# Turning filter rows with permutation matmuls instead of DRAM row moves, with later V loads and spread weight transposes

## Chip, cores, metric

The program runs on one core of one Trainium2 chip. The metric is the device time of one execution in microseconds (us). A ratio below is the mean time of one kernel's fast runs over that of the other's of the same rounds, so it is not quite the ratio of the medians quoted beside it.

## The reference, cut to what matters

```python
def _A_ref(x, w_r, w_i):                  # x: (1, 2048, 576)
    X = rfft2(x.astype(float32))          # (2048, 289) complex
    return irfft2(X * (w_r + 1j * w_i))   # filter: 2048 x 289

def _B_ref(x, w_gate, w_up, w_down):      # 576 -> 4608 -> 576
    return (gelu(x @ w_gate) * (x @ w_up)) @ w_down

g = sigmoid((x * gate_w).sum(-1))
out = g * _A_ref(x) + (1 - g) * _B_ref(x)
# wanted: out, and the gradients of x, w_r, w_i, w_gate, w_up, w_down, gate_w
```

The kernel does the Fourier transforms as matmuls. They are cut into small "units" and laid between the matmuls of the wide layer, so that TensorE (PE) always has work. The other engines are VectorE (DVE), ScalarE (ACT), GpSimd (POOL) and SyncE (SP), which issues the DMAs here.

## The kernel before

The wide layer has 18 groups of 256 hidden columns. Each group has four quarters (m = 0 to 3, 512 rows each), so there are 72 quarters; I count them from 0. A quarter begins with the matmuls `z` that read the transposed down-weights `wdT`.

By symmetry of the transform the kernel works on columns 0 to 144 of a row and meets columns 145 to 288 of the mirrored row there (row S - s for row s). So the right half of the filter has to be there in mirrored row order, and the right half of its gradient has to be put back. The kernel before does both through DRAM, on SP's queue:

```python
def reversed_rows(src, dst, tiles):
    s_, d_ = (a.rearrange("(m i) (h l) -> h i m l", i=T, h=2) for a in (src, dst))
    ...
    out.append(lambda i=i: LD.dma_start(d_[:, i], s_[:, T - i, ::-1]))   # LD = nc.sync
# main loop, end of a quarter
if m < 3 and g + 1 < NG:
    load_w(g + 1, m)            # part m of the next group's weights, also on SP
...
for _ in range(5 if pr < 8 else 2):
    if moves:
        moves.pop(0)()          # row moves, on SP
```

The middle of the transform, per pair of rows p, and the pool of "unit" buffers that it lives from (19 buffers, shared by everything named here):

```python
def prefetch(p):                # V tiles (vx, vg) and the filter tile W
    st[p, "vx"] = load_V(scr_x, i0); st[p, "vg"] = load_V(scr_g, i0)
    w = unit([2, 2, DF], name="Wt") ...
def s2(p, which, ii):           # last forward step: PE, then ACT, DVE
    ...
    if which == "g" and ii == 1:
        side.extend(products(p))        # 12 DVE items: m1 m2 qm n1 n2 qn o1 o2
        if p + 1 < T // 2: prefetch(p + 1)
def s1(p, key, ii, dst):        # first inverse step
    ...                                 # four matmuls into vps
    Vt = unit([2, 2, HF], name="Vt")    # a unit buffer
    nc.scalar.copy(Vt..., vps...)       # ACT drains PSUM
    LD.dma_start(dst..., Vt...)         # store
```

From group 1 on, `z` and all transform units share one PSUM buffer (pool `pz`, one buffer), which ACT drains; `da` is the tile that ACT writes when it drains `z`. Pairs of rows are worked on one after another: one turn of the middle takes the last forward steps of pair p and the first inverse steps of pair p - 1.

Of the kernel before, what the change touches and what calls it, by code (L numbers as in the profile page):

```python
# [9 lines left out]
ACT = mybir.ActivationFunctionType  # L10
# [53 lines left out]
def iotas(nc, res, unit):  # L64
    tb = Tables()
    G = nc.gpsimd
    kw = dict(allow_small_or_imprecise_dtypes=True)
    tb.lrow = unit([HF], F32, name="lrow")
    G.iota(tb.lrow[:], pattern=[[1, HF]], base=0, channel_multiplier=0, **kw)
    tb.dcol = res.tile([P, 5], F32, name="dcol")  # L70
    for par in range(2):
        G.iota(tb.dcol[:, 2 * par:2 * par + 2], pattern=[[256, 2]], base=par, channel_multiplier=2, **kw)
    G.iota(tb.dcol[:, 4:5], pattern=[[0, 1]], base=512, channel_multiplier=1, **kw)
    tb.dn = res.tile([P, 5], F32, name="dn")
    nc.vector.tensor_scalar(tb.dn[:], tb.dcol[:], 1.0 / D, None, op0=ALU.mult)
    tb.krow = res.tile([P, P], F32, name="krow")
    G.iota(tb.krow[:], pattern=[[1, P]], base=0, channel_multiplier=0, **kw)
    tb.scol = res.tile([P, T], F32, name="scol")
    G.iota(tb.scol[:], pattern=[[1, T]], base=0, channel_multiplier=16, **kw)
    tb.mrow_i = res.tile([P, P], I32, name="mrow_i")  # L80
    G.iota(tb.mrow_i[:], pattern=[[1, P]], base=0, channel_multiplier=0)
    tb.qcol_i = res.tile([P, 1], I32, name="qcol_i")
    G.iota(tb.qcol_i[:], pattern=[[0, 1]], base=0, channel_multiplier=1)
    par_i = res.tile([P, 1], I32, name="par_i")
    nc.vector.tensor_single_scalar(par_i[:], tb.qcol_i[:], 1, op=ALU.bitwise_and)
    tb.par = res.tile([P, 2], F32, name="par_f")
    nc.vector.tensor_copy(tb.par[:, 1:2], par_i[:])
    nc.vector.tensor_scalar(tb.par[:, 0:1], tb.par[:, 1:2], -1.0, 1.0, op0=ALU.mult, op1=ALU.add)
    tb.halfpi = res.tile([P, 1], F32, name="halfpi")
    nc.vector.memset(tb.halfpi[:], math.pi / 2)  # L90
    tb.pi = res.tile([P, 1], F32, name="pi")
    nc.vector.memset(tb.pi[:], math.pi * EPS_SCALE)
    tb.npi = res.tile([P, 1], F32, name="npi")
    nc.vector.memset(tb.npi[:], -math.pi * EPS_SCALE)
    tb.warm = res.tile([P, 1], F32, name="warm")
    nc.scalar.activation(tb.warm[:], tb.halfpi[:], ACT.Sin)
    tb.late = []
    tb.Dt = []
    return tb
# [86 lines left out]
def kernel(  # L186
# [22 lines left out]
    scr = [[dram.tile([TPB, P, FF], BF16, name=f"scr{k}_{tp}") for tp in range(NT)] for k in range(3)]  # L209
    a_scr = dram.tile([S, D], BF16, name="a_scr")  # L210
    dxa_scr = dram.tile([S, D], BF16, name="dxa_scr")
    wrev, orev = ([dram.tile([S, DF - HF], BF16, name=f"{n}{k}") for k in range(2)] for n in ("wrev", "orev"))
    scr_x = dram.tile([T, P, 2, 2 * HF], BF16, name="scr_x")
    scr_g = dram.tile([T, P, 2, 2 * HF], BF16, name="scr_g")
    scr_p1 = (dram.tile([T, P, 2, 256], BF16, name="scr_p1"), dram.tile([2, T, P, 2, NL // 2], BF16, name="scr_q1"))
# [45 lines left out]
        load_x(4 * k)  # L261
    for k in range(4):
        load_do(4 * k)
    for part in range(3):
        load_w(0, part)
    gwb = res.tile([P, D], BF16, name="gwb")

    ew = wstack.enter_context(tc.tile_pool(name="ew", bufs=2))
# [15 lines left out]
    omg32 = res.tile([P, T], F32, name="omg32")  # L284
    tb.Rt = []
    tb.At2 = hres.tile([P, 2, 2, 2 * HF], BF16, name="At2")
    tb.Oi = hres.tile([P, 2, HF], BF16, name="Oi")

    hctr = [0]
# [92 lines left out]
        V.tensor_tensor(q[:], xb[:], q[:], op=ALU.mult)  # L382
        return xb, q, s, hu

    stores, moves = [], []

    def flush(n=9):

# [156 lines left out]
    def tail_table():  # L545

        n = HF - P
        nc.gpsimd.memset(tb.At2[:], 0.0)
        tp_ = pz.tile([P, 2, 1024], BF16, tag="z", name="tp")
        for c in range(2):  # L550
            nc.tensor.transpose(tp_[:, c, 0:P], tb.Dt[2][:, c, 0:P], ident[:])
            nc.tensor.transpose(tp_[0:n, c, 256:256 + P], tb.Dt[2][:, c, P:HF], ident[:])
            nc.tensor.transpose(tp_[:, c, 512:512 + 32], tb.Dt[3][0:32, c, 0:P], ident[0:32, 0:32])
            nc.tensor.transpose(tp_[0:n, c, 768:768 + 32], tb.Dt[3][0:32, c, P:HF], ident[0:32, 0:32])
        V.tensor_copy(tb.Oi[:, :, 0:P], tp_[:, :, 0:P])
        V.tensor_copy(tb.Oi[:, :, P:HF], tp_[:, :, 512:512 + n])
        ot = unit([2, HF], name="ot")
        V.tensor_copy(ot[0:n, :, 0:P], tp_[0:n, :, 256:256 + P])
        V.tensor_copy(ot[0:n, :, P:HF], tp_[0:n, :, 768:768 + n])
        for i in range(2):  # L560
            LD.dma_start(tb.At2[i * NL:i * NL + n, i, :, 0:HF], tb.Dt[1][0:n])
            LD.dma_start(tb.At2[i * NL + n:(i + 1) * NL, i, :, HF:2 * HF], ot[0:n])
# [14 lines left out]
    wi_v = A_w_i.rearrange("(m i) l -> m i l", i=T)  # L577
    o2v = out_2.rearrange("(m i) l -> m i l", i=T)
    o3v = out_3.rearrange("(m i) l -> m i l", i=T)
    def tiles_of(t):  # L580
        return t[:].rearrange("(m i) l -> m i l", i=T)

    def reversed_rows(src, dst, tiles):

        s_, d_ = (a.rearrange("(m i) (h l) -> h i m l", i=T, h=2) for a in (src, dst))
        out = []
        for i in tiles:
            if i:
                out.append(lambda i=i: LD.dma_start(d_[:, i], s_[:, T - i, ::-1]))
            else:  # L590
                out.append(lambda: LD.dma_start(d_[:, 0, 1:P], s_[:, 0, P - 1:0:-1]))
                out.append(lambda: LD.dma_start(dst[0:1], src[0:1]))
        return out

    a_dv = a_scr[:].rearrange("(m i) d -> m i d", i=T)
    dxa_dv = dxa_scr[:].rearrange("(m i) d -> m i d", i=T)

    def mid_units():
        st = {}

        def prefetch(p):
            i0 = 2 * p
            st[p, "vx"] = load_V(scr_x, i0)
            st[p, "vg"] = load_V(scr_g, i0)
            w = unit([2, 2, DF], name="Wt")
            for k, v in enumerate((wr_v, wi_v)):
                LD.dma_start(w[:, k, :, 0:HF], v[:, i0:i0 + 2, 0:HF])
                LD.dma_start(w[:, k, :, HF:DF], tiles_of(wrev[k])[:, i0:i0 + 2, :])
            nc.gpsimd.tensor_scalar(w[:, 1, :, HF:DF], w[:, 1, :, HF:DF], -1.0, None, op0=ALU.mult)
            st[p, "w"] = w  # L610

        def s2(p, which, ii):
            def f():
# [14 lines left out]
                V.tensor_tensor(o[:, ii, :, DF - 1:HF - 1:-1], xe[:, :, 0:HF - 1], xe[:, :, HF:w - 1], op=ALU.subtract)  # L628
                if which == "g" and ii == 1:
                    side.extend(products(p))  # L630
                    if p + 1 < T // 2:
                        prefetch(p + 1)
            return f

        def products(p):
# [32 lines left out]
                return f  # L668

            def out_dw():  # L670
                o = st[p, "o1"]
                nc.gpsimd.tensor_scalar(o[:, :, 1, HF:DF], o[:, :, 1, HF:DF], -1.0, None, op0=ALU.mult)

                def store():
                    for k, v in enumerate((o2v, o3v)):
                        LD.dma_start(v[:, i0:i0 + 2, 0:HF], o[:, :, k, 0:HF])
                        LD.dma_start(tiles_of(orev[k])[:, i0:i0 + 2, :], o[:, :, k, HF:DF])
                        moves.extend(reversed_rows(orev[k][:], (out_2, out_3)[k][:, HF:DF], [(T - i) % T for i in (i0, i0 + 1)]))
                stores.append(store)
            return [  # L680
                lambda: halve(G),
                mul("m1", X, W[:, 0]), mul("m2", X, W[:, 1]), comb("m1", "m2", False),
# [6 lines left out]
        def s1(p, key, ii, dst):  # L689
            def f():  # L690
                i = 2 * p + ii
                while (p, key + "_q") not in st:
                    side.pop(0)()
                Pt = st[p, key + "_q"][:].rearrange("p i c e l -> p i c (e l)")
# [18 lines left out]
        NPAIR = T // 2  # L713
        for p in range(NPAIR + 1):
            if p < NPAIR:
                out += [s2(p, "x", 0), s2(p, "x", 1), s2(p, "g", 0), s2(p, "g", 1)]
            else:
                out += [gap] * 3
            if p > 0:
                out += [s1(p - 1, "m1", 0, scr_p1), s1(p - 1, "m1", 1, scr_p1)]  # L720
                out += [s1(p - 1, "n1", 0, scr_p2), s1(p - 1, "n1", 1, scr_p2)]
        return out

    def inv_units(s, dv, scale):
# [82 lines left out]
    run_late(tb)  # L807
    for t in range(T):
        x1[t]()
        if t % 4 == 2 and t < 14:  # L810
            tchunk(xn, xT, t + 2)
        if t >= 9 and t % 2 == 1:
            tchunk(dB, dOT, 2 * (t - 9))
        if t % 3 == 1 and t + 2 < T:
            build_R(nc, tb, unit, t + 2)
        if tb.late:
            tb.late.pop(0)()
        if t > 1:
            x2[t - 2]()
    x2[T - 2]()  # L820
    build_B(nc, tb, unit, res)
    run_late(tb)
    for i in range(T):
        for k, v in enumerate((A_w_r, A_w_i)):
            moves.extend(reversed_rows(v[:, HF:DF], wrev[k][:], [i]))
    x2[T - 1]()
    gate()

# [57 lines left out]
    for g in range(NG):  # L886
# [3 lines left out]
        for m in range(NPR):  # L890
# [4 lines left out]
            hs = [h for u in pend[m] for h in u] if pend else []  # L895

            def side_work():
                for _ in range(4):
                    if side:
                        side.pop(0)()  # L900
            if g == 0 and m > 0:
# [55 lines left out]
                LD.dma_start(gwb[:], gate_w.partition_broadcast(P))  # L957
            if (g, m) in ((0, 3), (1, 0)):
                scale_dB(T // 2)
            for _ in range(5 if pr < 8 else 2):  # L960
                if moves:
                    moves.pop(0)()
            assert pr != 8 or not moves
            if done[0] == n_slots or (pr >= wgT_from and pr % 2 == 0 and len(wgT_all) < 20):
                load_wgT()
                if done[0] == n_slots:
# [1 line left out]
        carry = pend[4] if pend else []  # L968
        pend = W_units(g)
    flush()  # L970
    assert fft_pos[0] == len(fft) and not side and not moves
    hstack.close()


# [225 lines left out]
```

## Time and profile before

| | before |
|---|---|
| time | 1493.15 us (1492.37 to 1493.29, 3 runs) |
| PE busy | 1413.8 us of 1492.2 |
| PE waits for `wdT` | 31.3 us, four times, at quarters 4 and 8 |
| PE waits behind ACT in the middle | 7.1 us for `da`, 5.7 us for `Vt` |

How to read it: what can be won is PE's idle time, and besides it the time that PE loses in matmuls at a low granted clock after a long wait ("slow clock" below), which the page counts as busy. The head is the time before quarter 0, the end stage that after the last quarter. A PE wait is listed with the engine, the tile and the line that ended it. "ACT Vt" means that PE waited for ACT to drain the transform's result and free the PSUM buffer. The lines are in the prediction.

### The profile page before, as it was taken

The numbers are of one execution on the slowest core, as the hardware profiler recorded it, in microseconds if no ns is written. First come the engines' busy times: TensorE is split into PE (matmuls) and PEld (weight loads), VectorE is DVE, ScalarE is ACT, GpSimd is POOL, SyncE is SP. The second block draws the span as 40 slices with busy tenths as digits, with TensorE's granted clock in tenths as the row PEclk, the third lists the DMA queues.
The fourth block names the chain that finished last, engine by engine and source line by source line (L and its number), as shares of the span: only waits on it lengthen the run. The fifth ranks groups of instructions, "written<-read, shape, count | busy, mean of one in ns | idle before, by whom it ended". The sixth has DMA issues, their size and how long they took to land.

```text
span 1492.2 us, 30025 instructions
## 1 busy us (share of the span) xinstructions
PE 1413.8 (95%) x11500; PEld 1050.0 (70%) x11586; DVE 886.3 (59%) x2356; ACT 695.5 (47%) x1380; POOL 136.1 (9%) x224
## 2 busy tenths in 40 slices
PE   7959599899999999999999999999999999999997
PEld 5637367666766676677777777777877777777776
DVE  6767277988888888876777777776000561212110
ACT  5846366576677666767677667664000000000000
POOL 1000011111111111010010010011000110000000
PEclk9979799999999999999999999999999999999999
DMA  5234364355555564456445546565999997877773
GB/s 194 67 85 104 92 183 135 105 122 144 137 135 135 137 158 110 116 135 152 122 124 141 151 125 163 142 155 138 268 208 200 209 211 159 167 161 163 156 153 73
DMA packets 555891, 217.63 MB, mean 146 GB/s; under 512 B 380868, under 2 KB 545860, under 8 KB 555748
## 3 DMA queue, kind: packets, MB, share of 16 engines
q1 hardware_dynamic: 546116, 195.21, 57.4%
q0 software_dynamic: 7824, 19.49, 4.5%
q8 instruction: 90, 1.47, 0.4%
q10 hardware_dynamic: 1808, 1.02, 0.3%
q14 instruction: 53, 0.43, 0.1%
HBM read 43.28 MB, written 96.22 MB: 93 GB/s over the span
## 4 chain that ended last, share of the span: by engine, by line
PE 57%; issue 0%; DVE 0%; ACT 0%; DVEq 0%
PE acc L1047 28%; PE wps L464 8%; PE xy L353 7%; PE wps L447 5%; PE z L341 4%; PE wps L477 1%; PE pf L748 1%; PE xy L348 1%; PE z L344 1%; PE pf L775 1%; PE pf L777 1%; PE pf L761 0%; ACT da L366 0%; DVE n L649 0%; PE pf L698 0%
## 5 line engine op out<-in xcount | busy, mean ns | idle before, releaser
L1047 PEld LDWEIGHTS <-pin 128*128 128x128 bf16 x3456 | 338.1, 98 | 85.1
L353 PE MATMUL xy<-wgu,xT 128*128 128x512 bf16 x1066 | 256.3, 379 | 10.6 <-issue 9.1
L464 PEld LDWEIGHTS <-xn 128*128 128x128 bf16 x2304 | 225.2, 98 | 31.2 <-issue 0.2
L353 PEld LDWEIGHTS <-xT 128*128 128x128 bf16 x1152 | 106.6, 98 | 138.8 <-issue 31.5
L366 ACT ACTIVATE da<-z,omg 128x256 bf16<-128x256 f32 x288 | 113.0, 474 | 150.0 <-PE z L344 147.1
L341 PE MATMUL z<-wdT,dOT 128*128 128x256 bf16 x1152 | 142.5, 278 | 37.6 <-DMA wdT<-wtmp 31.3
L1064 ACT COPY bo<-acc 128x288 f32<-128x288 f32 x32 | 12.7, 398 | 308.1 <-PE acc L1047 250.0
L341 PEld LDWEIGHTS <-dOT 128*128 128x128 bf16 x1152 | 112.8, 99 | 58.0 <-DMA wdT<-wtmp 32.1
L447 PE MATMUL wps<-dB,A 128*128 128x288 bf16 x1152 | 152.7, 286 | 0.0
L1047 PE MATMUL acc<-wgT,pin 128*128 128x288 bf16 x1152 | 143.6, 286 | 0.0
L1047 PE MATMUL acc<-wuT,pin 128*128 128x288 bf16 x1152 | 143.6, 286 | 0.0
L1047 PE MATMUL acc<-wd_all,pin 128*128 128x288 bf16 x1152 | 142.6, 286 | 0.0
L447 PEld LDWEIGHTS <-A 128*128 128x128 bf16 x1152 | 112.6, 98 | 34.9
L464 PE MATMUL wps<-dHg,xn 128*128 128x256 bf16 x1152 | 133.1, 273 | 0.0
L464 PE MATMUL wps<-dHu,xn 128*128 128x256 bf16 x1152 | 132.0, 273 | 0.0
L1124 DVE SCALAR_TENSOR_TENSOR f32t<-gwf,dlog,b16t 128x576 f32<-128x576 f32 x16 | 13.1, 818 | 176.7 <-DMA b16t<-dxa_scr 176.7
L372 ACT ACTIVATE q<-xy 128x512 bf16<-128x512 f32 x144 | 86.2, 598 | 65.8 <-PE xy L353 62.0
L396 ACT ACTIVATE om<-s 128x512 bf16<-128x512 bf16 x144 | 92.1, 640 | 22.6 <-DVE s L380 22.3
L397 ACT ACTIVATE s<-s 128x512 bf16<-128x512 bf16 x144 | 90.7, 630 | 4.6
L470 POOL DMA_DIRECT2D out_dram<-dw x67 | 48.9, 730 | 458.5 <-ACT dw L425 336.9
L379 DVE TENSOR_SCALAR s<-q 128x512 bf16<-128x512 bf16 x144 | 42.5, 295 | 80.8 <-ACT q L372 80.1
L378 ACT CAST hu<-xy 128x512 bf16<-128x512 f32 x144 | 87.2, 606 | 0.0
(209 smaller groups left out, 1803.9 us busy)
## 6 DMA issues: line engine op xcount, KB each, us to landing
scr<-A SPq DMA_DIRECT2D x144, 128.0 KB
scr<-dHg SPq DMA_DIRECT2D x144, 128.0 KB
scr<-dHu SPq DMA_DIRECT2D x144, 128.0 KB
out_dram<-dw POOLq DMA_DIRECT2D x67, 128.0 KB, 2.8
wd_all<-in_B_w_down_dram SPq DMA_DIRECT2D x3, 1728.0 KB
out_dram<-dwd POOLq DMA_DIRECT2D x34, 144.0 KB, 3.1
wgu<-in_B_w_gate_dram SPq DMA_DIRECT2D x18, 256.0 KB
wgu<-in_B_w_up_dram SPq DMA_DIRECT2D x18, 256.0 KB
```

What stands on the lines that cost most here:

```text
L341: nc.tensor.matmul(zo(t), lhsT=dOT[:, ci, t, :], rhs=wdT[:, ci, :], start=(t % 4 < 2 and ci == 0), stop=False)
L353: nc.tensor.matmul(xy[k][:, t % 2, :], lhsT=xT[:, ci, t, :], rhs=wgu[:, ci, :], start=False, stop=(ci == 3))
L366: nc.scalar.activation(da[:, tt, :], z[:, tt, k, :], ACT.Copy, scale=omg32[:, t:t + 1])
L372: nc.scalar.activation(q[:], xy[:, :, 0:FG], ACT.Square)
L378: nc.scalar.copy(hu[:], xy[:, :, FG:2 * FG])
L379: V.tensor_scalar(s[:], q[:], A_GELU, 1.0, op0=ALU.mult, op1=ALU.add)
L396: nc.scalar.activation(om[:], s[:], ACT.Sigmoid, scale=-2.0 * C_GELU)
L397: nc.scalar.activation(s[:], s[:], ACT.Sigmoid, scale=2.0 * C_GELU)
L447: nc.tensor.matmul(wps[:, :288], lhsT=tl(0, t)[:, fch * P:(fch + 1) * P], rhs=dB[:, t, h * 288:(h + 1) * 288], start=(t == 0), stop=(t == ...
L464: nc.tensor.matmul(wps[:, cc, :], lhsT=xn[:, t, (c0 + cc) * P:(c0 + cc + 1) * P], rhs=tl(k, t), start=(t == 0), stop=(t == T - 1))
L470: wst[0].dma_start(ov[:, c0:c0 + TPB, fsl], dw[:])
L1047: nc.tensor.matmul(acc[:, :288], lhsT=src[:, r, :], rhs=w_of(r)[:, h * 288:(h + 1) * 288], start=(first and r == 0), stop=(last and r == F ...
```

## The change

The intent: take the row moves out of SP's queue. Loads and stores fetch and put the mirrored row inside each block of 16 rows directly. Only the order of the 128 partitions is left to be turned, and a matmul with a permutation matrix J does that, in place (a "flip"). Beside this: weight transposes are issued later in the head, V and filter loads later, and the DVE side work goes three items at a time.

```diff
-    for part in range(3):
-        load_w(0, part)
+    load_w(0, 0)
 ...
+        if t in (6, 11):                       # in the head's loop
+            load_w(0, 1 + t // 11)
 ...
+        def flip(p, of):
+            ps = pftile()
+            for k in range(2):
+                for ii in range(2):
+                    nc.tensor.matmul(ps[:, k, ii * (HF - 1):(ii + 1) * (HF - 1)], lhsT=tb.J[:, int(p == ii == 0), :],
+                                     rhs=of(k)[:, ii if p == 0 else 1 - ii, HF:DF], start=(ii == 0), stop=(ii == 1))
+            for k in range(2):
+                nc.scalar.activation(of(k)[:, :, HF:DF], ps[...], ACT.Copy, scale=(1.0, -1.0)[k])
 ...
-                LD.dma_start(w[:, k, :, HF:DF], tiles_of(wrev[k])[:, i0:i0 + 2, :])
-            nc.gpsimd.tensor_scalar(w[:, 1, :, HF:DF], w[:, 1, :, HF:DF], -1.0, None, op0=ALU.mult)
+                for sb, d in mirrored(w[:, k], v, p):
+                    LD.dma_start(sb, d)
 ...
-                    if p + 1 < T // 2:          # in s2
+                    if p == 0:
                         prefetch(p + 1)
+                if key == "m1" and ii == 1 and p + 2 < T // 2:   # in s1
+                    prefetch(p + 2)
 ...
-                out += [s2(p, "x", 0), s2(p, "x", 1), s2(p, "g", 0), s2(p, "g", 1)]
+                out += [flip_w(p), s2(p, "x", 0), s2(p, "x", 1), s2(p, "g", 0), s2(p, "g", 1)]
 ...                                             # and flip_o(p - 1) after the four s1
-                for _ in range(4):              # side_work
+                for _ in range(3):
 ...
-            for _ in range(5 if pr < 8 else 2):
-                if moves:
-                    moves.pop(0)()
```

More of the change, by code (lines that the diff above doesn't have):

```diff
@@ L88, in iotas @@
     nc.vector.tensor_scalar(tb.par[:, 0:1], tb.par[:, 1:2], -1.0, 1.0, op0=ALU.mult, op1=ALU.add)
+    tb.rcol = res.tile([P, 2], F32, name="rcol")
+    G.iota(tb.rcol[:], pattern=[[1, 2]], base=P - 1, channel_multiplier=-1, **kw)
     tb.halfpi = res.tile([P, 1], F32, name="halfpi")
@@ L211 @@
     dxa_scr = dram.tile([S, D], BF16, name="dxa_scr")
-    wrev, orev = ([dram.tile([S, DF - HF], BF16, name=f"{n}{k}") for k in range(2)] for n in ("wrev", "orev"))
     scr_x = dram.tile([T, P, 2, 2 * HF], BF16, name="scr_x")
@@ L286 @@
     tb.At2 = hres.tile([P, 2, 2, 2 * HF], BF16, name="At2")
+    tb.J = hres.tile([P, 2, P], BF16, name="J")
     tb.Oi = hres.tile([P, 2, HF], BF16, name="Oi")
@@ L383, in H_ew1 @@
         return xb, q, s, hu
-    stores, moves = [], []
+    stores = []
     def flush(n=9):
@@ L548, in tail_table @@
         nc.gpsimd.memset(tb.At2[:], 0.0)
+        for k in range(2):
+            V.tensor_scalar(tb.J[:, k, :], tb.krow[:], tb.rcol[:, k:k + 1], None, op0=ALU.is_equal)
+        nc.gpsimd.memset(tb.J[0:1, 1, 0:1], 1.0)
         tp_ = pz.tile([P, 2, 1024], BF16, tag="z", name="tp")
@@ L579 @@
     o3v = out_3.rearrange("(m i) l -> m i l", i=T)
-    def tiles_of(t):
-        return t[:].rearrange("(m i) l -> m i l", i=T)
-    def reversed_rows(src, dst, tiles):
-        s_, d_ = (a.rearrange("(m i) (h l) -> h i m l", i=T, h=2) for a in (src, dst))
-        out = []
-        for i in tiles:
-            if i:
-                out.append(lambda i=i: LD.dma_start(d_[:, i], s_[:, T - i, ::-1]))
-            else:
-                out.append(lambda: LD.dma_start(d_[:, 0, 1:P], s_[:, 0, P - 1:0:-1]))
-                out.append(lambda: LD.dma_start(dst[0:1], src[0:1]))
-        return out
     a_dv = a_scr[:].rearrange("(m i) d -> m i d", i=T)
@@ L599, in mid_units, with mirrored, flip_w, flip_o @@
         st = {}
+        def mirrored(sb, v, p):
+            hi = slice(HF, DF)
+            if p == 0:
+                return [(sb[:, 0, hi], v[:, 0, hi]), (sb[:, 1, hi], v[:, T - 1, hi])]
+            return [(sb[:, :, hi], v[:, T - 1 - 2 * p:T + 1 - 2 * p, hi])]
+        def flip(p, of):
[4 more added lines that the diff above has]
+                                     rhs=of(k)[:, ii if p == 0 else 1 - ii, HF:DF], start=(ii == 0), stop=(ii == 1))
+            for k in range(2):
+                nc.scalar.activation(of(k)[:, :, HF:DF], ps[:, k, :DF - 1].rearrange("p (i l) -> p i l", i=2), ACT.Copy,
+                                     scale=(1.0, -1.0)[k])
+        def flip_w(p):
+            return lambda: flip(p, lambda k: st[p, "w"][:, k])
+        def flip_o(p):
+            def f():
+                while (p, "o1_ready") not in st:
+                    side.pop(0)()
+                o = st[p, "o1"]
+                flip(p, lambda k: o[:, :, k, :])
+                def store():
+                    for k, v in enumerate((o2v, o3v)):
+                        LD.dma_start(v[:, 2 * p:2 * p + 2, 0:HF], o[:, :, k, 0:HF])
+                        for sb, d in mirrored(o[:, :, k, :], v, p):
+                            LD.dma_start(d, sb)
+                stores.append(store)
+            return f
         def prefetch(p):
@@ L630, in f @@
                     side.extend(products(p))
-                    if p + 1 < T // 2:
+                    if p == 0:
                         prefetch(p + 1)
@@ L670, in out_dw @@
             def out_dw():
-                o = st[p, "o1"]
-                nc.gpsimd.tensor_scalar(o[:, :, 1, HF:DF], o[:, :, 1, HF:DF], -1.0, None, op0=ALU.mult)
-                def store():
-                    for k, v in enumerate((o2v, o3v)):
-                        LD.dma_start(v[:, i0:i0 + 2, 0:HF], o[:, :, k, 0:HF])
-                        LD.dma_start(tiles_of(orev[k])[:, i0:i0 + 2, :], o[:, :, k, HF:DF])
-                        moves.extend(reversed_rows(orev[k][:], (out_2, out_3)[k][:, HF:DF], [(T - i) % T for i in (i0, i0 + 1)]))
-                stores.append(store)
+                st[p, "o1_ready"] = True
             return [
@@ L720, in mid_units @@
                 out += [s1(p - 1, "m1", 0, scr_p1), s1(p - 1, "m1", 1, scr_p1)]
-                out += [s1(p - 1, "n1", 0, scr_p2), s1(p - 1, "n1", 1, scr_p2)]
+                out += [s1(p - 1, "n1", 0, scr_p2), s1(p - 1, "n1", 1, scr_p2), flip_o(p - 1)]
         return out
@@ L822 @@
     run_late(tb)
-    for i in range(T):
-        for k, v in enumerate((A_w_r, A_w_i)):
-            moves.extend(reversed_rows(v[:, HF:DF], wrev[k][:], [i]))
     x2[T - 1]()
@@ L959 @@
                 scale_dB(T // 2)
-            for _ in range(5 if pr < 8 else 2):
-                if moves:
-                    moves.pop(0)()
-            assert pr != 8 or not moves
             if done[0] == n_slots or (pr >= wgT_from and pr % 2 == 0 and len(wgT_all) < 20):
@@ L970 @@
     flush()
-    assert fft_pos[0] == len(fft) and not side and not moves
+    assert fft_pos[0] == len(fft) and not side
     hstack.close()
```

## The prediction

> **What bounds the kernel now.** I read the page first, then the list of waits, then the timeline of PE around each gap, then the DMA issues of SP in the same gap.
>
> ```profile
> PE 1413.8 (95%) x11500; PEld 1050.0 (70%) x11586; DVE 886.3 (59%) x2356; ACT 695.5 (47%) x1380; POOL 136.1 (9%) x224
> PE   7959599899999999999999999999999999999997
> PEclk9979799999999999999999999999999999999999
> ```
>
> PE is the bound: 1413.8 of 1492.2 us, so 78 us at most can be won without removing matmuls. The weak slices are the first six (37.3 us each), so nearly all that can be won lies before 220 us. The list of waits names the largest one; columns are total us, times, longest:
>
> ```profile
> PE z L341 <- DMA wdT<-wtmp: 31.3, 4, 15.9
> ```
>
> PE waits 31.3 us for the transposed down-weights of the next group of 256 hidden columns. Narrowed to 40 to 230 us it is all there: a wait of 14.14 (and 0.64) us that ends at 103.3 and 104.5, when group 1 starts, and one of 15.89 (and 0.61) us at 178.5 and 179.7, when group 2 starts. No later group waits. What holds the weights up is seen in the timeline of SP (start, us, engine, line) beside that of PE:
>
> ```profile
> 157.67 1.29 SPq L242 DMA_TRANSPOSE wtmp<-in_B_w_down_dram  x1
> 159.00 0.63 SPq L589 DMA_DIRECT2D wrev<-in_A_w_i_dram  x1
> ...
> 165.28 3.10 SPq L589 DMA_DIRECT2D wrev<-in_A_w_i_dram  x1
> 168.49 2.33 SPq L412 DMA_DIRECT2D scr<-A  x1
> ...
> 174.98 0.54 SPq L245 DMA_DIRECT2D wdT<-wdT  x1
> 175.57 2.63 SPq L248 DMA_DIRECT2D wdT<-wtmp  x4
> ```
> ```profile
> 178.45 0.59 PE L341 MATMUL z<-wdT,dOT 128*128 128x256 bf16 x2 [15.89 <-DMA wdT<-wtmp]
> 179.65 3.15 PE L341 MATMUL z<-wdT,dOT 128*128 128x256 bf16 x14 [0.61 <-DMA wdT<-wtmp]
> ```
>
> (The second fence has PE lines alone.) All three parts of a weight load are on one in-order queue with the moves that reverse the filter rows (wrev, L589) and all stores. There are 34 such issues, most of them a median 2.2 or 2.6 us each on SP, five in every quarter group from 68 to 185 us. The queue thus falls some 16 us behind PE.
>
> **What the skill says.** "DMA: Bandwidth & Descriptors", section "Anatomy of one DMA", says that DMA engines do not wait on semaphores, the wait sits on the issuing sequencer before dispatch. The trace agrees: the copies at 174.98 stand behind everything issued before them. "TensorE: Matmul & The Clock Gate", Part 1, says an idle window drops the array to half clock until it has been busy again for about 3.4 us. The trace agrees:
>
> ```profile
> 160.00:170.00 10.00, 2.56 (x24) 2.05 (x21) 3.35 (x9) 0.00 (x0) 2.21 (x3) 0.85 0.27 52
> 170.00:180.00 10.00, 0.93 (x4) 0.49 (x5) 0.00 (x0) 0.00 (x0) 0.00 (x0) 0.50 0.52 141
> ```
>
> (Columns: stretch, length, busy us and count of PE, PEld, DVE, ACT, POOL, then granted clock, DMA share, GB/s.) The clock is 0.50, and 14 matmuls take 3.15 us where 16 take 1.91 elsewhere. So a long gap costs more than itself. The same page, "Back-to-back issue gap", gives N/2.4 + 2.5 ns per warm matmul. For 256 columns that is 109 ns; the chain of work has 16 in 1.75 us, 109 each, so it agrees, and I use it for the new matmuls.
>
> **The change, part by part.**
>
> 1. Moves gone. All 34 row moves of the filter and 34 of the gradient (median 0.73 us) leave SP; loads and stores fetch the mirrored rows directly, and what is still to do, turning the partitions round, goes to PE. For group 2 the copies then follow the transposes one quarter later as in later groups: group 3's were issued at 218.02, 13 us before they are needed at 230.02. The second stall vanishes whole. The quarter begins at 162.5 and ends at 192.41, 29.9 us. Its work without waits: 13.96 us from 178.45, less 2.75 of slow clock (9.9 us from its z to the end of its second xy, 7.15 in the next quarter), is 11.2. **Gain 18.5 us.**
>
> 2. Group 1's stall. The copies follow the stores of the third quarter. DVE, 9.4 us busy of each 10 us here, ends that quarter's first half at 84.0. Then about 0.5 us, 0.54 + 2.65 us of issue, and some 1.5 us to landing (the last copy was issued by 103.05, its wait ended at 104.52): about 89.2. PE arrives at 89.1, so the DMA wait goes to 0 to 1 us. But DVE finishes the fourth quarter only at 97.2, and scales the gradient until 99.5; PE wants its results, or the z buffer they hold, from about 94.5 on. I allow 2 us of waiting for that. Before, the quarter took 119.67 - 89.1 = 30.6; the next quarter, 133.19 - 119.67, shows 13.5 without waits. 30.6 - 13.5 - 2 = **gain 15 us.**
>
> 3. Head. The weight parts (L242 to L248) hold SP until 24.9, so that the first V store starts only at 25.0, and DVE and PE run out of buffers:
>
> ```profile
> 25.00 27.21 SPq L541 DMA_DIRECT2D scr_x<-Vt  x16
> 27.48 0.36 DVE L146 TENSOR_SCALAR CR<-XR 128x384 int32<-128x384 int32 x1 [3.48 <-DMA scr_x<-Vt]
> ```
> ```profile
> 29.23 1.11 PE L303 MATMUL tp<-ident,dB 128*128 128x128 bf16 x16 [2.97 <-DVE Vt L538]
> ```
>
> Spreading the transposes to the steps t = 6 and t = 11 takes this away: 2.97 us, and up to 1.6 us of slow matmuls behind it (1.66 for 0.91, 1.12 for 0.66, 1.45 for 1.05). The copies still come long before 49.4, where they are wanted. Other engines may take part of it back. **Gain 3.5 us.**
>
> 4. Middle. Two kinds of PE wait are there now:
>
> ```profile
> 299.59 3.02 PE L341 MATMUL z<-wdT,dOT 128*128 128x256 bf16 x16 [4.51 <-ACT Vt L703]
> ```
> ```profile
> 466.40 0.28 PE L698 MATMUL pf<-qn,Rt 128*128 128x290 bf16 x1 [1.41 <-ACT da L366]
> ```
>
> The first comes once: the evicting ACT waits for a unit buffer whose last reader is a DVE product. V loads half a turn later keep two V buffers and one W buffer free, and side work goes three at a time instead of four. Gap and slow clock behind it (3.02 for 1.91, 0.61 for 0.39) make about 6 us. **Gain 6 us.** The second comes in five pairs of rows, 7.1 us in all: a burst of four DVE items (from 458.6 to 462.8 around 466) delays ACT, and the single z buffer is not drained. With three in a burst the worst is n, combine and fold, o: 0.75 + 0.93 + 1.01 + 0.75 = 3.4 us instead of 4.7 (fold, two products, combine and fold). I take **2 us** of 7.1.
>
> 5. Added on PE: 16 flips of four matmuls, 144 columns. By the skill's form each is 144/2.4 + 2.5 = 62.5 ns; the weight load row says 98 ns. An estimate between, about 85 ns, gives 0.34 us a flip. **Cost 5.5 us**, all on the path, PE being full there.
>
> 6. Added on ACT: 32 evictions of 128x288, which by the bo row (398 ns) and dwd (0.38 to 0.45) are 0.4 us, 13 us in all. ACT is 69 of 100 us busy in the middle, so none of it is on the path by itself; but the flip sits in the single z buffer for 0.8 us and more. I allow 0.2 us of PE waiting for each of 16 flips. **Cost 3.2 us.** The two POOL negations (0.93 and 0.98 us, eight each) go, which stands beside other work.
>
> Sum: -18.5 - 15 - 3.5 - 6 - 2 + 5.5 + 3.2 = -36.3, from 1493.15 to 1457.
>
> The end stage, from about 1040 us, has PE at 20.00 of 20.00 us and nothing in it changes: what is won early should arrive whole.
>
> **Rivals.** (a) DVE takes the stall's place. It is 9 tenths busy from 60 to 97 us. For it: its backlog of 8 us at 89. Against it: from 110 to 163 it needs 39 us in four quarters, 9.8 us of 13.5 to 15, so it catches up. At the worst the first stall gives 9 instead of 15: 1463. (b) The z buffer becomes the bound in the middle. The schedule places the units by load; from the code, the middle grows from 70 to 86 slots, from two per quarter to two or three. For it: the five waits of 1.4 us. If each flip waits 1 us and the old waits stay: 16 - 3.2 + 2 = 14.8 more, 1472. Against it: behind 690 us three and four units per quarter go with no PE wait listed. (c) A flip waits for its filter rows. They come only three slots before it, and the second pair's one slot. Against it: SP's loads for the second pair were issued from 248.1 to 251.1 while PE took their slot at 259.4. If it happens, 2 us for each of eight pairs, 1473. (d) All goes well: middle waits vanish, flips cost 65 ns a matmul and wait for nothing: 1457 - 5.1 - 1.3 - 3.2 = 1447.
>
> **Range and chances.** The two stalls are 33.5 us of the 36.3 and are the surest, since the moves leave the queue whatever else happens. The rest are small terms of either sign, each with a doubt of 2 to 5 us. So 1457 with 1448 to 1469. Faster by 2% means below 1463.3: that fails only with rival (b) or (c), or with (a) and another small loss. 0.82 faster, 0.17 within, 0.01 slower.
>
> **What would show it.** Right: the wait of z for wdT falls from 31.3 us to under 2; slices 3 and 5 of the clock row are 9; SP shows V stores from about 17 us on; the flips' matmuls last under 100 ns from start to start. Part 4: no gap over 2 us at the first pair. Wrong: new PE waits on an ACT eviction of a flip, or on a DMA into Wt, of more than 5 us in all, or a wait of PE for DVE's dHg over 4 us near 95 us. If PE's gaps close and the time stays, my claim that PE time arrives at the end undiminished is false.

## The result, and the profile after

1470.01 us, median of 4 runs (1468.49 to 1471.21), against 1493.22 us before; the ratio is 0.9844 (0.9827 to 0.9861). I had said 1457, with 1448 to 1469, and gave 0.82 to a gain of more than 2%. The gain is 23 us (1.6%) instead of 36.

The page of the changed kernel, the same three rows as before:

```profile
PE 1416.7 (96%) x11564; PEld 1053.2 (72%) x11650; DVE 881.3 (60%) x2355; ACT 707.3 (48%) x1415; POOL 121.0 (8%) x210
PE   7989999999898999999999999999999999999997
PEclk9999999999999999999999999999999999999999
```

The weak slices 3 and 5 are gone and the granted clock is 9 throughout. But PE's idle time is still 1468.1 - 1416.7 = 51.4 us, where it was 78.4.

The stalls on `wdT`. First SP's DMA issues, then PE's line for the z of quarter 8 (start, us, engine, line):

```profile
131.95 0.51 SPq L246 DMA_DIRECT2D wdT<-wdT  x1
132.52 2.65 SPq L249 DMA_DIRECT2D wdT<-wtmp  x4
```
```profile
146.62 1.91 PE L342 MATMUL z<-wdT,dOT 128*128 128x256 bf16 x16
```

The copies are issued from 131.95 to 135.2, and z reads them at 146.62, 11 us after the last; it starts with no wait in brackets, and its 16 matmuls take 1.91 us, as elsewhere without a wait.

What is new is in the list of PE's waits (total us, times, longest):

```profile
PE z L342 <- ACT Vt L722: 8.5, 2, 5.9
...
PE pf L717 <- ACT Vt L722: 3.8, 1, 3.8
PE pf L602 <- DMA Wt<-in_A_w_r_dram: 2.8, 1, 2.8
...
PE acc L1061 <- DMA pin<-scr: 1.7, 1, 1.7
```

No `wdT` is in it. Instead PE waits 12.3 us for ACT to drain `Vt`, which was 5.7 us before, and 2.8 us for the filter rows of one flip.

**Where the gain was made and lost.** The start of each quarter's z in the two traces gives the lead of the changed kernel:

| start of | before | after | lead |
|---|---|---|---|
| quarter 0 (end of the head) | 49.44 | 46.63 | 2.8 |
| quarter 5 | 119.67 | 102.53 | 17.1 |
| quarter 10 | 205.01 | 168.11 | 36.9 |
| quarter 13 | 242.52 | 206.37 | 36.2 |
| quarter 14 | 255.03 | 223.92 | 31.1 |
| quarter 25 | 406.91 | 371.31 | 35.6 |
| quarter 26 | 421.00 | 390.35 | 30.7 |
| quarter 31 | 487.51 | 463.23 | 24.3 |
| quarter 71 (the last) | 1019.58 | 993.73 | 25.9 |
| the end of the span | 1492.2 | 1468.1 | 24.1 |

By quarter 10 the kernel had won 36.9 us; my first three parts had promised 15 + 18.5 + 3.5 = 37. The rest of the change had to keep that, and did not: three steps down (quarter 13: 5.0 us; quarter 25: 5.0; quarters 29 and 30: 6.5) take 16.5 us, and only part of it is won back elsewhere.

The two later steps have one form. These lines of the timeline are DVE's, ACT's and PE's, in order of start, in quarter 29 and at the start of quarter 30:

```profile
447.26 0.76 DVE L674 TENSOR_TENSOR n<-Xg,Wt 128x1156 bf16<-128x1156 bf16 x1
...
448.11 0.64 ACT L722 CAST Vt<-pf 128x580 bf16<-128x580 f32 x1 [6.88 <-DVE n L674]
...
448.80 3.57 PE L342 MATMUL z<-wdT,dOT 128*128 128x256 bf16 x16 [5.92 <-ACT Vt L722]
```

ACT stands idle for 6.88 us before it drains a PSUM result that is ready, because the buffer `Vt` it is to write into was last the filter tile W of the next pair (by the code and the releaser; the trace leaves buffer numbers out), and DVE has yet to do the product `n` that reads it. DVE gets to it at 447.26. PE waits for the PSUM buffer behind ACT, and then runs 16 matmuls in 3.57 us instead of 1.91. ACT's own list has the waits of this form as its largest entry for `Vt`:

```profile
ACT Vt L722 <- DVE n L674: 11.9, 3, 6.9
```

(Four more waits of ACT for `Vt`, 8.9 us, end with other DVE steps; the PE wait of 2.6 us at quarter 17 stands behind one of these, a combine of `n`, and not behind a product of the filter tile as the expectation of vt_in_q has it.)

So theory A: **the loss is a hand-over of unit buffers.** The program gives `Vt` a buffer that DVE has not released, since DVE runs some microseconds behind PE. Its rival B: DVE's lateness itself is the cause, and without this buffer PE would meet it a moment later at another wait, as it did before at `da`. For the flips, theory C: a flip costs only its matmuls, and one waits for its rows. Rival D: they also hold the single PSUM buffer.

The cost of a flip can be read from the starts of PE's lines:

```profile
585.64 0.41 PE L602 MATMUL pf<-Wt,J 128*128 128x144 bf16 x4
585.89 3.65 PE L465 MATMUL wps<-dHu,xn 128*128 128x256 bf16 x32
```

From start to start it is 0.25 us for four, 62.5 ns each, or 4.0 us for 16 flips; I had taken 5.5.

### The profile page after: what moved, and what is told of

It reads as the page before. It is cut to its first block, busy times and chain, and to the rows that moved or that the text cites. A ratio compares the mean times of both kernels' runs of the same rounds, so it can differ in the third digit from the quotient of the medians.

```text
span 1468.1 us, 30087 instructions
## 1 busy us (share of the span) xinstructions
PE 1416.7 (96%) x11564; PEld 1053.2 (72%) x11650; DVE 881.3 (60%) x2355; ACT 707.3 (48%) x1415; POOL 121.0 (8%) x210
## 4 chain that ended last, share of the span: by engine, by line
PE 71%; DVE 2%; DMA 1%; issue 1%; SPq 0%; ACT 0%; DVEq 0%; ACTq 0%
PE acc L1061 28%; PE wps L465 12%; PE xy L354 11%; PE wps L448 7%; PE z L342 6%; PE wps L478 2%; PE xy L349 1%; PE z L345 1%; PE pf L767 1%; DMA pin<-scr 1%; PE pf L794 1%; PE pf L796 1%; SPq L1026 0%; PE pf L780 0%; DVE n L674 0%
## 5 line engine op out<-in xcount | busy, mean ns | idle before, releaser
L1078 ACT COPY bo<-acc 128x288 f32<-128x288 f32 x32 | 12.8, 399 | 310.4 <-PE acc L1061 310.4
L465 PE MATMUL wps<-dHg,xn 128*128 128x256 bf16 x1152 | 136.6, 275 | 0.0
L381 DVE TENSOR_TENSOR s<-xb,s 128x512 bf16<-128x512 bf16 x144 | 61.3, 426 | 39.1 <-ACT xb L378 31.7
```

The source lines that it names most:

```text
L381: V.tensor_tensor(s[:], xb[:], s[:], op=ALU.mult)
L465: nc.tensor.matmul(wps[:, cc, :], lhsT=xn[:, t, (c0 + cc) * P:(c0 + cc + 1) * P], rhs=tl(k, t), start=(t == 0), stop=(t == T - 1))
```

## The experiments

Twelve runs in three calls, each call on a chip of its own with runs of the kernel before beside it: median 1491.56 us in the first (7 runs), 1497.95 (1494.3 to 1501.28) in the second, 1492.44 in the third. In the second call the kernel before was slower than elsewhere, so its ratios flatter; I compare those runs with one another and by the quarters of their traces. The lengths of quarters without a PE wait hardly vary: where two programs do the same thing, they agree to a few hundredths of a us in different runs. Those with a wait vary more: quarter 25 of the changed kernel itself lasts 19.0 us in its first trace and 17.9 in after_again.

### First call: which part costs what

**vt_in_q: no buffer for Vt.** `s1` writes into the half of `qm` or `qn` that its matmuls have just read. The result is correct.

```diff
-                Vt = unit([2, 2, HF], name="Vt")
-                nc.scalar.copy(Vt[:].rearrange("p c e l -> p c (e l)"), vps[:, :, :w])
+                Vt = st[p, key + "_q"][:, ii]
+                nc.scalar.copy(Vt.rearrange("p c e l -> p c (e l)"), vps[:, :, :w])
```

> The changed kernel, but the inverse transform's first step writes its result back into the tile that it has just read, instead of taking a unit buffer of its own (Vt). Theory A (a buffer wait): in the changed kernel ACT waits three times, 11.9 us in all, for a unit buffer whose last reader is the DVE product of the filter tile, and PE waits 2.58, 3.79 and 5.92 us behind it, with some 3 us of slow clock after: without the buffer these go and the time falls by 12 to 16 us, to about 1456. Theory B (DVE's backlog): ACT and PE would meet the late DVE products a moment later at another wait (the z buffer behind da, as in the kernel before, 1.4 us each): the time falls by at most 4 us, to 1466 to 1470.

Measured: 1456.32 us (1454.41 to 1457.24, 4 runs), ratio 0.9756; the changed kernel has 0.9844. That is 13 to 14 us faster, in the middle of what A expected and far from B. What is left in its list of PE waits (the largest that belong to the middle):

```profile
PE pf L717 <- ACT da L367: 3.0, 1, 3.0
...
PE pf L602 <- DMA Wt<-in_A_w_r_dram: 2.5, 1, 2.5
```

Of the waits for a `Vt` of the inverse step (now named `qm` or `qn`) 0.2 us are left. Quarters 25 and 29 last 13.0 us each, where they lasted 19.0 and 19.1. B holds in one place only: quarter 17, in the first pair, grows from 13.2 to 17.3 us, with the 3.0 us wait on `da` above. One rival stays: the edit also takes four tiles a pair out of the pool, so a larger pool might have served as well. No run tests that.

**side4: four side items per call again.**

```diff
-                for _ in range(3):
+                for _ in range(4):
```

> The changed kernel with four side items per call again instead of three. My prediction's step (bursts of DVE delay ACT's da): slower by 3 to 6 us, five waits of PE on da of about 1.4 us come back, 1474. Theory A (the buffer waits come because the last product on the filter tile now sits in a later, smaller portion close before the eviction that takes its buffer): the waits of 3.79 and 5.92 us go or shrink, faster by 5 us or more, 1464 or less.

Measured: 1467.41 us (1464.29 to 1471.72), ratio 0.9837: the time is the same within the spread, so neither expectation of it is met. Its PE waits:

```profile
PE z L342 <- ACT Vt L722: 7.5, 4, 2.8
...
PE pf L717 <- ACT da L367: 0.9, 2, 0.4
```

The waits on `da`, 7.1 us in the kernel before, do not come back with portions of four. So the step of my prediction that put them down to bursts of four is not supported; they went with some other part of the change. The two large `Vt` waits shrink, as A said (3.8 to 1.3 us, 5.9 to 2.7), but others come: PE's waits for `Vt` are still 9.3 us. Quarters 25 and 29 get shorter by 4.0 and 2.6 us, quarter 33 longer by 3.0.

**early_pf: V and filter loads where the kernel before had them.**

```diff
-                    if p == 0:
+                    if p + 1 < T // 2:
                         prefetch(p + 1)
 ...
-                if key == "m1" and ii == 1 and p + 2 < T // 2:
-                    prefetch(p + 2)
```

> The changed kernel with the V and filter loads of the next pair issued where the kernel before issued them (at the last step of the pair before) instead of half a turn later. If the late loads are what frees buffers, as I predicted, then this has more buffer waits: slower by 3 to 10 us, 1473 to 1480. If the late loads do not matter, 1469 to 1471. If they are what makes the buffers change hands badly, faster by 5 us or more.

Measured: 1463.68 us (1460.11 to 1464.94), ratio 0.9806: some 6 us faster than the whole change. Its `Vt` waits are 7.8 us instead of 12.3:

```profile
PE z L342 <- ACT Vt L720: 4.0, 2, 2.5
PE pf L715 <- ACT Vt L720: 3.8, 1, 3.8
```

The late loads do not relieve the pool, they harm it here. Quarter 29 falls from 19.1 to 14.7 and quarter 30 from 14.4 to 12.7, quarter 25 stays at 19.0. At quarter 29 ACT now waits 2.5 us for a store to release the buffer, so another buffer is handed on. The pool is tight: in a check off the chip the changed kernel passes with 18 buffers, deadlocks with 17, and with 20 its tiles no longer fit. So of 19 there is hardly a spare one to take in place of one still in use.

**no_flip: the flips left empty**, their places kept (filter half wrong).

```diff
         def flip(p, of):
+            return
```

> The changed kernel with the 16 flips left empty, their places in the schedule kept; results of the filter half are wrong on purpose. By the trace a flip takes PE 0.25 us, 4.0 us in all; the second pair's flip waits 2.95 us for its filter rows and costs some 2 us of slow clock. Theory C (flips cost only that): 1470 less 4 less 5, about 1461. Theory D (flips hold the single z buffer and cost PE another 0.2 to 1 us each, rival b of the prediction): 1445 to 1457.

Measured: 1459.61 us (1459.05 to 1460.79), ratio 0.9784, some 9 us faster than the change. That is C: 4.0 us of matmuls and the 5 us step of quarter 13, which falls from 17.6 to 12.5 us. D's share is not to be seen, though the `Vt` waits are 14.0 us in this run instead of 12.3, behind which up to 2 us of it could hide:

```profile
PE z L342 <- ACT Vt L724: 8.7, 2, 5.9
PE pf L719 <- ACT Vt L724: 5.3, 2, 3.8
```

### Second call: the kernel before, with one part each

**b_no_moves: the kernel before without the row moves** (filter half wrong).

```diff
-            moves.extend(reversed_rows(v[:, HF:DF], wrev[k][:], [i]))
 ...
-                LD.dma_start(w[:, k, :, HF:DF], tiles_of(wrev[k])[:, i0:i0 + 2, :])
+                LD.dma_start(w[:, k, :, HF:DF], v[:, i0:i0 + 2, HF:DF])
 ...                                             # the same for the stores
```

> The kernel before with all 68 row moves taken out and the filter and gradient halves loaded and stored unturned (results of the filter half wrong on purpose). By the traces the two stalls of group 1 and 2 gave 13.3 and 19.7 us: if the moves alone made them, the time falls by 31 to 35 us to about 1460. Rival (the earlier weight transposes or the later V loads have a share in it): falls by less than 28 us.

Measured: 1461.21 us (1460.76 to 1463.44), ratio 0.9751: 36.7 us below the slower runs of before. By the spans of the two traces, of different chips, it is 1492.2 - 1459.0 = 33.2 us, as expected. The moves alone made both stalls: quarters 3 and 4 together fall from 39.6 to 25.3 us, 7 and 8 from 44.8 to 25.7. What PE waits for in its middle:

```profile
PE pf L697 <- ACT da L366: 10.4, 7, 1.8
...
PE z L341 <- ACT Vt L702: 3.2, 1, 3.2
```

So taking the moves away is worth more than the whole change; the middle of the change, flips and buffers together, gives some of it back.

**b_spread: the kernel before with only the weight transposes spread.**

```diff
-    for part in range(3):
-        load_w(0, part)
+    load_w(0, 0)
 ...
+        if t in (6, 11):
+            load_w(0, 1 + t // 11)
```

> The kernel before with only the weight transposes spread over the head. The trace of the changed kernel is 2.8 us ahead at the first z: expected -2 to -3 us, 1490 to 1491, if the lead passes through the stalls. If the stalls (bound by SP's queue) swallow it: 0 to -1 us.

Measured: 1494.23 us (1493.03 to 1496.47), ratio 0.997 (0.9953 to 0.9988). The first z starts at 44.76 instead of 49.44, and of these 4.7 us 3.8 are left at the last quarter. A little more than expected; part of it can be chance, as b_no_moves, with the head of the kernel before, has its first z at 48.21. The stalls (31.8 us here) do not swallow it.

**w1_early: the second pair's filter rows loaded earlier.**

```diff
+            if p != 1:
+                prefetch_w(p)
+        def prefetch_w(p):
             w = unit([2, 2, DF], name="Wt")
 ...                                             # in s2
+                if p == 0 and which == "x" and ii == 1:
+                    prefetch_w(1)
```

> The changed kernel with the second pair's filter rows loaded some two slots earlier. Its flip then does not wait (2.79 and 0.16 us) and the slow clock behind it goes: expected -4 us, 1466, if nothing takes its place; 0 if the buffer taken earlier makes another wait.

Measured: 1467.45 us (1465.04 to 1469.71). Quarter 13 falls from 17.6 to 12.8 us, but quarter 16 grows from 15.3 to 17.0, and PE's waits for `Vt` from 12.3 to 14.0: a buffer taken earlier makes another hand-over late. From the first to the last quarter 2.7 us are left against the changed kernel, of 4 expected.

**vt_in_q_w1: both.**

> Both: no Vt buffer in the inverse transform's first step, and the second pair's filter rows earlier. Theory A: -12 to -16 and -4 add up, about 1452 us, faster than both kernels. Theory B: 1463 to 1466.

Measured: 1455.82 us (1455.19 to 1459.65), 11.6 us faster than w1_early on the same chip, but not the 1452 that A gave for both together. Quarter 13 is 12.8, quarters 25 and 29 are 13.0, but quarter 17 is now 21.3. Two lines of its timeline show what is there, DVE's and PE's:

```profile
262.39 0.84 DVE L697 TENSOR_TENSOR qn<-n 128x576 bf16<-128x576 bf16 x2 [1.88 <-DMA scr_p<-qn]
...
267.53 0.40 PE L724 MATMUL pf<-qn,Rt 128*128 128x290 bf16 x1 [5.71 <-ACT da L367]
```

A fold on DVE waits 1.88 us for a store to release a buffer, as `qm` and `qn` are now held until they are stored; DVE falls further behind, and PE waits 5.71 us. So of the two gains about 4 us more than in vt_in_q were given back in the first pair.

### Third call: the changed kernel again, and three attempts on what is left

**after_again: the changed kernel unaltered.**

> The changed kernel once more, unaltered, on the chip of the three runs beside it: 0.984 of the kernel before, as at first, and the same three ACT waits for a unit buffer held by a DVE product of the filter tile (11.9 us).

Measured: 1470.49 us (1467.99 to 1471.55), ratio 0.9849. Its trace lists the same 11.9 us of ACT.

**vtq_w1_side4: vt_in_q_w1 with four side items per call.**

> No Vt buffer, second pair's filter rows early, and four side items per call. What remains in the middle after the first two edits is one wait of PE of 5.7 us at the first pair, behind a late DVE. If it is a product that comes too late (portions of three), four at a time shortens it: -3 to -6 us against the version with three, 0.968 of before. If it is DVE's whole backlog, the bursts of four bring 1.4 us waits back in the later pairs: +2 to +6 us.

Measured: 1456.57 us (1454.22 to 1457.3), ratio 0.9755. Neither expectation is met: quarter 17 falls from 21.3 to 14.1, but quarters 13, 14, 21 and 25 grow by 2.7, 1.6, 1.4 and 1.8.

**vtq_w1_reuse: two products written into dead tiles.**

```diff
-                    st[p, key] = unit([2, 2, DF], name=key)
+                    old = {"n1": "m2", "o1": "n2"}.get(key)
+                    st[p, key] = st[p, old] if old else unit([2, 2, DF], name=key)
```

> No Vt buffer, second pair's filter rows early, and two of eight product tiles of a pair (n1, o1) written into dead ones (m2, n2) of the same engine, so that 15 instead of 17 buffers of a pair change hands. Theory A: the wait of DVE on a store (1.88 us) and of PE behind it (5.7 us) at the first pair go: -4 to -7 us, 0.968 of before. If the backlog of DVE at the first pair is the cause by itself: no change.

Measured: 1454.12 us (1452.13 to 1454.95), ratio 0.9743. Quarter 17 is 18.7 instead of 21.3, so the hand-over was 2.6 us of it, less than A gave. PE still waits 4.3 us on `da`. The lines at this wait, ACT's and PE's, show what is behind it:

```profile
263.13 0.63 ACT L397 ACTIVATE om<-s 128x512 bf16<-128x512 bf16 x1 [4.28 <-DVE s L381]
...
265.94 0.39 PE L725 MATMUL pf<-qn,Rt 128*128 128x290 bf16 x1 [4.31 <-ACT da L367]
```

ACT stands 4.28 us before another step that needs a result of DVE, and so drains `z` late. DVE itself waits only 0.48 us for a store in this stretch. The larger part is thus DVE's lateness at the first pair, as far as the trace shows; no run removes it.

**vtq_w1_early: vt_in_q_w1 with the loads where the kernel before had them.**

> No Vt buffer, second pair's filter rows early, and V loads where the kernel before had them. With Vt gone from the pool the late loads should no longer matter in the later pairs: equal within 2 us to the version with late loads (0.972 of before), apart from the first pair, where a wait may come or go by up to 5 us.

Measured: 1452.55 us (1451.21 to 1453.46), ratio 0.9730 (0.9716 to 0.9745), correct: the lowest median of all (vtq_w1_reuse is within its spread), 18 us faster than the change on the same chip and 40 us faster than before. From quarter 25 on it has the lengths of the version with late loads (13.0 in 25 and 29), so with `Vt` out of the pool the place of the loads no longer matters there, as expected. What differs is quarter 17, 19.0 instead of 21.3. Its page and the one wait of the middle that is left:

```profile
PE 1411.3 (97%) x11564; PEld 1050.5 (72%) x11650; DVE 881.2 (61%) x2355; ACT 706.5 (49%) x1415; POOL 120.5 (8%) x210
```
```profile
PE pf L722 <- ACT da L367: 3.8, 1, 3.8
```

## Why the prediction was right or wrong

**Part 1 (moves gone), part 2 (group 1), part 3 (head): right.** Together 37 promised, 36.9 us of lead measured at quarter 10: 19.3 in quarters 7 and 8 (18.5 promised, and my own sum there gives 18.7), 14.3 in quarters 3 and 4 (15), 2.8 in the head (3.5; 4.3 in after_again), and 0.5 in quarters with other units than before. That the total is so close is in part luck. In b_no_moves, which has the same units per quarter as before, the quarter I worked out at 11.2 us (quarter 8) lasts 10.9, and the one for which I allowed 15.5 (quarter 4) lasts 15.4. The DVE backlog of rival (a), for which I allowed 2 us, shows in quarter 4 as three waits of under 1 us each, 2.4 us in all, and no more.

**Part 4 (middle): wrong, and this is the step that failed.** I said that the late V loads keep two V buffers and one W buffer free, so that ACT's wait for a unit buffer goes, gain 6 us, and that portions of three win another 2 us. Neither reason stands. The wait of the first pair went down only from 4.5 to 2.6 us and two larger ones came, in quarters 25 and 29: with slow clock they cost 5.0 and 6.5 us against before. early_pf shows that the late loads cost 6 us where I booked a gain (nor are they half a turn later: they come 7 to 18 us later, in turns of some 60); vt_in_q shows that the buffer of `Vt` is what 13 to 14 us hang on. The 1.4 us waits on `da` did go (7.1 to 0.5 us), which is more than I booked, but side4 shows that it was not for the reason I gave. My mistake was to count how many buffers are free. What mattered was from which engine the next buffer comes, and how far that engine runs behind. My list of signs would not have caught it: the wait for `wdT` went, the clock row is 9, the V stores start at 17.32, and waits for flips or for their rows stayed at 3 us; only "no gap over 2 us at the first pair" failed, by 0.6.

**Part 5 (flips on PE): mechanism right, size off.** 62.5 ns a matmul, 4.0 us in all instead of 5.5. The form N/2.4 + 2.5 was right as it stood, and the mixture with the weight load row was not needed. (The page gives that form for an isolated matmul, which the prediction left out; see the last section.)

**Part 6 (flips hold the z buffer): not seen.** I booked 3.2 us; no_flip leaves at most some 2 us for it beyond the matmuls and quarter 13.

**Rival (c) came true once, and I had ruled it out too soon.** The second pair's flip waited 2.8 us for its rows, with slow clock and one more unit in that quarter 5.0 us in all. I argued that SP had issued these loads 8 us before PE took the slot, but that was read from the old schedule. In the new one the last filter load is issued at 214.63 and PE is there at 214.1 (216.86 less its wait of 2.79):

```profile
214.63 0.47 SPq L634 DMA_DIRECT2D Wt<-in_A_w_i_dram  x1
```
```profile
216.86 0.35 PE L602 MATMUL pf<-Wt,J 128*128 128x144 bf16 x2 [2.79 <-DMA Wt<-in_A_w_r_dram]
```

The other pairs did not wait.

**"What is won early should arrive whole": off by 1.8 us.** From the last quarter to the end it takes 472.6 us before and 474.4 after, with one new PE wait on `pin<-scr`. In the other runs it is 473.2 to 479.0 us, with PE waits on `pin<-scr` of 0 to 3.7 us. An earlier start alone does not explain it: no_flip starts this stage 9 us earlier than the change and has no such wait. The cause stays open.

The sum of the misses: steps that I had as a loss of about 0.7 us (part 4, 5, 6 together, 8 won and 8.7 paid) came out as a loss of 36.9 - 25.9 = 11.0 us, and the end stage took 1.8 more. That is the 12 to 13 us between 1457 and 1470.

**Still open:** why the `da` waits vanished (side4, early_pf and no_flip each undo one part, and in none of them do they come back to more than 0.9 us; all three keep the larger number of steps, which no run changes alone); what makes DVE late in quarter 17; and why some runs of the head are 1.5 us shorter (the first z at 46.6 or at 45.1 for the same program).

## What to carry to other kernels

A long run of small DMA issues on an in-order queue delays what stands behind it. Here the 34 gradient moves, spread thinly, held nothing up that PE waited for, and the 34 filter moves, five a quarter, cost both stalls: look for loads that PE waits for, and read what was issued before them. In a shared pool of buffers, ask for each new tile whose buffer it will get and which engine has to let go of it; a drain of PSUM should not hang on an engine that runs behind. Writing a result back into a tile that has just been read by the same step takes a tile out of the pool. It was worth more here than moving loads about, though the tile written to is then held until it is stored (quarter 17 grew by 4.2 us).

## What the Trainium skill lacked or had wrong

- "TensorE: Matmul & The Clock Gate", section "Back-to-back issue gap", gives a sustained spacing in real kernels of about 81 ns at N = 128 and 131 ns at N = 512, with weight loads, and calls N/2.4 + 2.5 the isolated case. Here, with a weight load for every matmul, 144 columns take 62.5 ns (0.25 us for four) and 512 columns 216 ns (the chain of work of the kernel before has eight in 1.73 us). Both are N/2.4 + 2.5.
- "DMA: Bandwidth & Descriptors", section "Issuing engines are not separate DMA queues", says that the issue time saved by another engine is usually small relative to the DMA. That section does not say that a queue that falls behind holds up everything after it: here 34 issues, most of a median 2.2 or 2.6 us, held two weight loads back, and PE for 31.3 us.
- No page was found that has the hand-over of a pool's buffers between engines that run at different distances behind PE (a tile for which there is no room, as a cause of repeated bubbles, is as near as they come): 11.9 us of ACT waiting in three places, and 13 to 14 us of the time without that buffer.
